# A sliding-window attention and gated MLP block: one task graph with a list scheduler in place of a hand-written order, GELU from one table function, LayerNorm by bn_stats with its small steps on GpSimd

## The chip, the cores and the metric

The kernel runs on one core of a Trainium2 chip. The core has TensorE (PE, matmuls; PEld is its weight loads), VectorE (DVE), ScalarE (ACT), GpSimd (POOL) and SyncE (SP), which here issues every transfer. Each engine works through its own queue in order and waits on semaphores for the others. The metric is device time of one execution in microseconds (us); the median of the runs shown stands for the kernel.

## What is computed

The reference, cut to what matters (S = 2048 tokens, D = 448, 16 heads of 28, F = 1792, Fh = 896; bfloat16 in and out):

```python
h  = x + A(layernorm(x))
h2 = h + B(layernorm(h))                  # the output

def A(x):                                 # 16 heads, Dh = 28, W = 8, dilation 2
    q, k, v = split(x @ wqkv)
    # query t sees keys t, t-2, ..., t-14 (those >= 0)
    logits = where(mask, einsum(q, k[window]) * Dh**-0.5, -1e9)
    return einsum(softmax(logits), v[window]) @ wo

def B(x):
    z  = gelu(x @ w_in)                   # tanh form
    z1 = z[..., :Fh]
    z2 = layernorm(z[..., Fh:])
    g  = w_sp @ z2 + b_sp[:, None]        # mixes the tokens, 2048 x 2048
    return (z1 * g) @ w_out
```

## The kernel before

Tokens lie in 16 blocks of 128 (`x_tm`, one row per token). A LayerNorm scales a block into `tring`, PE transposes it, and the result goes into `xhT` (features on the partitions). Attention runs over 18 blocks of 114 queries with 14 keys of history, so that a block's window is a band of 128 keys: logits for 16 heads into four PSUM banks (L416), exponentials on ACT (L423) into `E`, a mask by DVE (L432), the product with V and a column of ones for the denominator (L444), division (L454, L457), transpose (L472, L475), output projection and residual (L485, L488).

The order is written out by hand. First come statistics of x (L347, L348), one rsqrt chain of 16 DVE operations for eight blocks at a time (`rsqrt_chain`), scaling on DVE (L351), and the q and k projections of tokens 0 to 1023 (L383). A loop over attention blocks then interleaves logits, V, products and outputs, with two "fillers" in each round: the remaining q and k tiles and transposes. Only when all 16 blocks of h exist (its sums are collected by L488 and L491) does the second LayerNorm begin: sums to mean and variance, the rsqrt chain, 16 scalings (L351), 64 transposes (L360) with 16 copies (L369).

The MLP follows: 32 half tiles of z2 (L744), each with GELU spelled out as copy from PSUM (L708, ACT), three DVE operations (L712 to L714), a sigmoid (L718, ACT), a product with a running sum (L723, DVE) and a square with a running sum (L733, ACT). After the last of them come the third LayerNorm's chain and 16 in-place scalings of `z2p` (L787). Then 28 tiles (7 feature chunks by 4 token chunks of 512), each with z1 (L755, the same GELU with L727 at its end), 16 accumulating matmuls for g (L800), bias and product (L813, L815); behind each token chunk four output blocks (L823, L827, and the store L829). `w_sp` is held transposed as two halves of 1024 tokens: `wspT_lo` is loaded at the start (L309), `wspT_hi` where the attention's buffers were, once these are free (L668).

The class `Sched` only turns reads and writes into semaphore waits; what stands first in the program stands first in an engine's queue.

Of the kernel before, what the change touches and what calls it, by code (L numbers as in the profile page):

```python
# [1 line left out]

# [27 lines left out]
GELU_C = 0.044715  # L30
GELU_K2 = 1.5957691216057308
RSQ_MAGIC = 0x5F3759DF
# [9 lines left out]
class Res:  # L42
    __slots__ = ("name", "writes", "reads", "prewritten")

    def __init__(self, name, prewritten=False):
        self.name = name
        self.writes = {}
        self.reads = {}
        self.prewritten = prewritten


class Sched:
    EXEC_ENGS = ("pe", "act", "dve", "pool", "sp")

    def __init__(self, nc):
        self.nc = nc
# [7 lines left out]
        self.store_keys = []  # L64

    def issue(self, exe, fn, reads=(), writes=(), prod=None, inc=1):
        if prod is None:
            prod = exe
        elif prod == "dma":
            prod = "q%d" % self.ndma  # L70
            self.ndma += 1
            self.keys.append(prod)
        needed = {}
        for r in reads:
            assert r.writes or r.prewritten, "read of never-written resource " + r.name
            for e, c in r.writes.items():
                if c > needed.get(e, 0):
                    needed[e] = c
        for w in writes:
            for e, c in w.writes.items():  # L80
                if c > needed.get(e, 0):
                    needed[e] = c
            for e, c in w.reads.items():
                if c > needed.get(e, 0):
# [3 lines left out]
        for e, c in needed.items():  # L88
# [5 lines left out]
            snap = self.hist[e][c]  # L94
            for k, v in snap.items():
# [9 lines left out]
        for r in reads:  # L105
            r.reads[prod] = n
        for w in writes:
            w.writes = {prod: n}
            w.reads = {}
        self.ops[exe].append((waits, fn, prod, inc))  # L110
        return prod, n

    def wait_keys(self, exe, keys):
        self.ops[exe].append(([(k, self.cnt[k]) for k in keys], None, None, 0))

    def emit(self, exe, eng):
        sems = self.sems
        for waits, fn, prod, inc in self.ops[exe]:
            for e, c in waits:
                eng.wait_ge(sems[e], c * 16 if e.startswith("q") else c)  # L120
            if fn is None:
                continue
            ins = fn(eng)
            if prod is not None:
                ins.then_inc(sems[prod], inc)


def bass_sequential_preLN__sliding_local_dilated__mixer_gmlp__prompt_kernel(
# [11 lines left out]
    sch = Sched(nc)  # L140
    iss = sch.issue

    X = A_x[0]
    OUT = out[0]

    with contextlib.ExitStack() as top:
        def sb(name, shape, dt, es=top):
            return es.enter_context(nc.sbuf_tensor(name, shape, dt))

        x_tm = sb("x_tm", [128, NB, D], BF16)  # L150
        NTR = 8
# [4 lines left out]
        ones1 = sb("ones1", [1, 128], BF16)  # L156
        bsp = sb("bsp", [1, S_TOK], BF16)
        bb = sb("bb", [128, S_TOK], BF16)
        warm = sb("warm", [128, 512], BF16)
        mf = sb("mf", [128, 128], F32)  # L160
        ij = sb("ij", [128, 128], I32)
        pf = sb("pf", [128, 128], F32)
        st1 = sb("st1", [128, NB, 6], F32)
        mv1 = sb("mv1", [128, NB, 2], F32)
        s2a = sb("s2a", [128, NB], F32)
        s2b = sb("s2b", [128, NB], F32)
        s3a = sb("s3a", [128, 2, NB], F32)
        s3b = sb("s3b", [128, 2, NB], F32)
        junk = sb("junk", [128, 512], BF16)
        junk2 = sb("junk2", [128, 512], BF16)  # L170
        mv2 = sb("mv2", [128, NB, 2], F32)
        mv3 = sb("mv3", [128, NB, 2], F32)
        rsa = [sb("rsa%d" % i, [128, NB], F32) for i in range(4)]
        rsti = [sb("rsi%d" % i, [128, NB], I32) for i in range(4)]
        rsy = [sb("rsy%d" % i, [128, NB], F32) for i in range(4)]
        rst1 = [sb("rst%d" % i, [128, NB], F32) for i in range(4)]
        w_in = sb("w_in", [DC, NCH, F_DIM], BF16)
        wspT_lo = sb("wspT_lo", [128, NB, 1024], BF16)

# [4 lines left out]
        r_tr = [Res("tring%d" % s) for s in range(NTR)]  # L184
        r_xhT = [Res("xhT%d" % m) for m in range(NB)]
        r_xhTpad = Res("xhTpad")
# [707 lines left out]
```

## Time and profile before

| | us |
|---|---|
| median of the two runs shown | 345.44 (345.01 and 345.88) |
| span of the profiled execution, first to last instruction | 342.4 |
| median less span | 3.0 |
| mean granted TensorE clock of the profiled execution | 0.915 |

The two runs are given as whole times only; of the profiled execution the span is what is known, so the difference stands for what lies around it. The page's parts are the busy time of each engine, the span in 40 slices with the granted clock, the chain of work that ended last, and groups of instructions by source line; a table of stretches gives the same busy times between two moments, and a timeline single instructions. A name such as L744 is a line of the kernel before.

### The profile page before, as it was taken

Reading aid. Unit: us, or ns where it says so; the run is one execution under the profiler, and the core shown is the slowest. Engines: PE = TensorE matmul, PEld = TensorE weight load, DVE = VectorE, ACT = ScalarE, POOL = GpSimd, SP = SyncE. Lnnn points to the kernel's source line nnn. Section 1 sums busy time; section 2 is a strip of 40 time slices with the busy share of each in tenths; the row PEclk is TensorE's granted clock in tenths of the full one; section 3 lists DMA queues with packets and bytes.
Section 4 is the critical chain, followed back from the end, with each engine's and each line's share of the span. In section 5 each row is a group of like instructions: output and inputs, shape, how many; then the busy total and the mean of one; then the engine's idle time right before and its main releaser. Section 6 shows DMA issues by size and latency. Waiting matters only on the chain.

```text
span 342.4 us, 4998 instructions
## 1 busy us (share of the span) xinstructions
PE 287.6 (84%) x1859; PEld 144.9 (42%) x1872; DVE 242.8 (71%) x670; ACT 156.8 (46%) x320; POOL 5.1 (1%) x17
## 2 busy tenths in 40 slices
PE   3789899999998848966550099999999999999996
PEld 1434455555565617521110034444444444444442
DVE  4987446897779779899999896554555565545554
ACT  1435878777866020899999322221222022212220
POOL 5000000000000000000000000000000000000000
PEclk9879989999987556999996589999999999999999
DMA  7999900000000069930000000001000100000001
GB/s 223 258 220 179 190 16 2 2 0 2 3 2 1 2 162 187 161 76 0 0 1 1 0 2 0 0 2 50 3 3 0 38 17 0 0 26 30 1 0 54
DMA packets 40537, 16.39 MB, mean 48 GB/s; under 512 B 34177, under 2 KB 39617, under 8 KB 40514
## 3 DMA queue, kind: packets, MB, share of 16 engines
q1 hardware_dynamic: 40514, 16.08, 22.5%
q8 instruction: 14, 0.23, 0.3%
q14 instruction: 9, 0.07, 0.1%
HBM read 5.85 MB, written 1.84 MB: 22 GB/s over the span
## 4 chain that ended last, share of the span: by engine, by line
PE 66%; DVE 28%; ACT 2%; issue 2%; DMA 1%; ACTq 0%; DVEq 0%
PE psum L800 29%; PE psum L383 9%; PE psum L755 7%; PE psum L823 6%; DVE z2p L723 5%; PE psum L400 4%; PE psum L485 4%; PE psum L444 4%; DVE wk L714 3%; DVE wk L712 3%; DVE wk L713 3%; DVE xhT L369 2%; DVE tring L351 2%; PE psum L416 2%; DVE st L347 1%
## 5 line engine op out<-in xcount | busy, mean ns | idle before, releaser
L708 ACT ACTIVATE xb<-psum 128x448 bf16<-128x448 f32 (+1 forms) x60 | 33.4, 558 | 108.3 <-PE psum L755 95.5
L800 PE MATMUL psum<-wspT_lo,z2p 128*128 128x512 bf16 x217 | 52.7, 388 | 17.9 <-DVE z2p L787 17.4
L712 DVE TENSOR_TENSOR wk<-xb 128x448 bf16<-128x448 bf16 (+1 forms) x60 | 24.2, 404 | 40.1 <-ACT xb L708 40.1
L800 PE MATMUL psum<-wspT_hi,z2p 128*128 128x512 bf16 x218 | 49.7, 379 | 0.3
L423 ACT ACTIVATE E<-psum 128x456 bf16<-128x456 f32 (+1 forms) x72 | 39.6, 550 | 15.1 <-PE psum L472 8.8
L800 PEld LDWEIGHTS psum<-wspT_lo,z2p 128*128 128x128 bf16 x224 | 21.9, 98 | 46.9 <-DVE z2p L787 22.3
L718 ACT ACTIVATE tb<-wk 128x448 bf16<-128x448 bf16 (+1 forms) x60 | 35.9, 598 | 12.7 <-DVE wk L714 12.7
L744 PE MATMUL psum<-w_in,xhT 112*128 112x448 bf16 x128 | 28.7, 365 | 11.1 <-ACT xb L708 11.1
L800 PEld LDWEIGHTS psum<-wspT_hi,z2p 128*128 128x128 bf16 x224 | 21.9, 98 | 26.5
L755 PE MATMUL psum<-xhT,w_in 112*128 112x512 bf16 x112 | 28.8, 379 | 1.2 <-ACT xb L708 1.2
L714 DVE TENSOR_TENSOR wk<-wk,xb 128x448 bf16<-128x448 bf16 (+1 forms) x60 | 24.5, 408 | 2.1
L744 PEld LDWEIGHTS psum<-w_in,xhT 112*128 112x128 bf16 x128 | 11.4, 101 | 28.0 <-ACT xb L708 19.0
L444 PEld LDWEIGHTS psum<-V,E 128*114 128x114 bf16 (+1 forms) x288 | 21.4, 149 | 2.4 <-issue 0.4
L823 PE MATMUL psum<-w_out,z1p 128*128 128x448 bf16 x112 | 22.0, 353 | 0.1
L444 PE MATMUL psum<-V,E 128*114 128x29 bf16 (+1 forms) x288 | 21.7, 210 | 0.0
L485 PE MATMUL psum<-wo,OT 112*128 112x448 bf16 x64 | 18.4, 420 | 3.9 <-DVE OT L475 2.8
L432 DVE TENSOR_TENSOR E<-E,maskb 128x1824 bf16<-128x1824 bf16 (+1 forms) x18 | 19.9, 1103 | 1.8 <-ACT E L423 1.7
L813 DVE TENSOR_TENSOR ub<-psum,bb 128x512 bf16<-128x512 f32 x28 | 19.1, 683 | 2.3 <-PE psum L800 2.3
L723 DVE CUSTOM_DVE_ANT_0 z2p<-tb,xb 128x448 bf16<-128x448 bf16 x32 | 19.8, 618 | 0.9 <-ACT tb L718 0.8
L383 PE MATMUL psum<-xhT,wqp 112*128 112x512 bf16 x64 | 18.1, 440 | 2.3 <-DVE xhT L369 2.3
L827 DVE TENSOR_TENSOR tring<-psum,x_tm 128x448 bf16<-128x448 f32 x16 | 10.0, 624 | 13.5 <-PE psum L823 13.5
L713 DVE TENSOR_SCALAR wk<-wk 128x448 bf16<-128x448 bf16 (+1 forms) x60 | 17.1, 285 | 2.1
(82 smaller groups left out, 338.1 us busy)
## 6 DMA issues: line engine op xcount, KB each, us to landing
x_tm<-in_A_x_dram SPq DMA_DIRECT2D x4, 448.0 KB, 7.2
out_dram<-tring SPq DMA_DIRECT2D x16, 112.0 KB, 1.7
w_in<-in_B_w_in_dram SPq DMA_DIRECT2D x1, 1568.0 KB, 15.5
stg<-in_A_wqkv_dram SPq DMA_DIRECT2D x1, 1176.0 KB, 9.9
w_out<-in_B_w_out_dram SPq DMA_DIRECT2D x1, 784.0 KB, 4.5
wo<-in_A_wo_dram SPq DMA_DIRECT2D x1, 392.0 KB, 12.9
wspT_lo<-in_B_w_sp_dram SPq DMA_TRANSPOSE x16, 4.0
wspT_hi<-in_B_w_sp_dram SPq DMA_TRANSPOSE x16, 4.1
```

What stands on the lines that cost most here:

```text
L383: e.matmul(out_ap, wsrc[:, c, gg, :], xhT[0:DC, c, col0:col0 + 512], start=(c == 0), stop=(c == NCH - 1)),
L423: iss("act", lambda e, in_ap=in_ap, out_e=out_e: e.activation(out_e, in_ap, AF.Exp, scale=SCALE), reads=[r_bank[hh]], writes=[r_E[slot]])
L444: e.matmul(psum[0:nq, ob + h * 32: ob + h * 32 + DH + 1], E[0:nk, slot, eidx, 0:nq], V1[0:nk, vslot, h, 0:DH + 1]),
L708: iss("act", lambda e: e.activation(self.XB, self.in_ps_ap, AF.Copy), reads=[self.rbank], writes=[r_xb[s]])
L712: iss("dve", lambda e: e.tensor_tensor(self.WK, self.XB, self.XB, ALU.mult), reads=[r_xb[s]], writes=[r_wk[s]])
L714: iss("dve", lambda e: e.tensor_tensor(self.WK, self.WK, self.XB, ALU.mult), reads=[r_wk[s], r_xb[s]], writes=[r_wk[s]])
L718: iss("act", lambda e: e.activation(self.TB, self.WK, AF.Sigmoid, scale=GELU_K2), reads=[r_wk[s]], writes=[r_tb[s]])
L723: iss("dve", lambda e: e.tensor_tensor_reduce(self.out_dst_ap, self.TB, self.XB, 1.0, 0.0, ALU.mult, ALU.add, self.sum_x_ap), reads=[r_tb[ ...
L744: iss("pe", lambda e, c=c: e.matmul(out_ap, xhT[0:DC, c, PAD + 128 * m: PAD + 128 * m + 128], w_in[:, c, FH + D * k: FH + D * (k + 1)], st ...
L755: iss("pe", lambda e, c=c: e.matmul(out_ap, w_in[:, c, fc * 128:(fc + 1) * 128], xhT[0:DC, c, PAD + 512 * tc: PAD + 512 * (tc + 1)], start ...
L800: iss("pe", lambda e, sbk=sbk: e.matmul(out_ap, z2p[:, sbk, fc * 128:(fc + 1) * 128], wsrc[:, sbk, coff:coff + 512], start=(sbk == 0), sto ...
L823: iss("pe", lambda e, fc=fc: e.matmul(out_ap, z1p[:, fc, 128 * m:128 * m + 128], w_out[:, fc, :], start=(fc == 0), stop=(fc == FC7 - 1)), ...
```

## The change

Every piece of work becomes a task of a graph: alternatives of engine and duration, the buffers that it reads, writes or adds to, and a priority. `Graph.schedule` places the tasks one at a time: among the tasks whose inputs are planned it takes the engine that can start first, and on it, of those that could start within 0.05 us, the one of the lowest priority number; buffers of a pool (PSUM banks, rings) are assigned then. The queues are written in the order of the planned starts, so waits are again only semaphores, but the order comes from these durations:

```diff
+LAT = {"pe": 0.20, "act": 0.16, "dve": 0.14, "pool": 0.20, "sp": 0.0}
+TABLE_US = 1.4
...
+            eng = min(first, key=lambda e: first[e])
+            lim = first[eng] + 0.05
+            best = min((c for c in by_task.values() if c[3] == eng and c[0] <= lim), key=lambda c: (c[2].prio, c[2].idx))
...
+        def pe_us(n, cols):
+            return n * (cols / 2400.0 + 0.003)
+        def act_us(n, sbuf=False):
+            return (n + (190 if sbuf else 105)) / 1200.0
+        def dve_us(n, rate=1.0):
+            return (n / rate + 85) / 960.0
```

All three LayerNorms go block by block, by `bn_stats` and `bn_aggr` on DVE; the variance plus epsilon and its power -0.5 go to GpSimd, and for the first two LayerNorms the scaling too:

```diff
+        def layernorm(m, i, prio):
+            G.add([("dve", dve_us(D))], [lambda e: e.bn_stats(st[:, s.slot, 0:6], x_tm[:, m, :])],
...
+            rstd_of(k, prio)
...
+            G.add([("pool", 0.65)], [lambda e: e.tensor_scalar(tring[:, t.slot, :], x_tm[:, m, :], mv[:, k, 0:1],
+                                                              rstd[:, k:k + 1], ALU.subtract, ALU.mult)],
...
+            G.add([("act", act_us(512)), ("dve", dve_us(512, 2))], [evac], [b], [r_xhT[m]], prio=prio)
...
+        def rstd_of(k, prio):
+            G.add([("pool", 0.2)], [lambda e: e.tensor_scalar(va[:, k:k + 1], mv[:, k, 1:2], EPS, None, ALU.add)],
...
+            G.add([("pool", 0.3)], [lambda e: e.tensor_tensor(rstd[:, k:k + 1], va[:, k:k + 1], mhalf[:, 0:1], ALU.pow)],
-            iss("dve", lambda e: e.tensor_tensor_reduce(x_tm[:, m, :], out_ap, x_tm[:, m, :], 1.0, 0.0,
-                                                       ALU.add, ALU.add, s2a[:, m:m + 1]),
...
+            G.add([("dve", dve_us(D))], [lambda e: e.tensor_tensor(x_tm[:, m, :], bank(b, D), x_tm[:, m, :], ALU.add)],
+                  [b, r_x[m]], [r_x[m]], prio=p)
+            layernorm(m, 1, p + 0.3)
```

GELU is one ACT operation from PSUM for z2 and z1; a z2 half tile may start on PE behind the fourth-last exponential, its GELU behind the last:

```diff
-                iss("act", lambda e: e.activation(self.XB, self.in_ps_ap, AF.Copy), reads=[self.rbank], writes=[r_xb[s]])
-                iss("dve", lambda e: e.tensor_tensor(self.WK, self.XB, self.XB, ALU.mult), reads=[r_xb[s]], writes=[r_wk[s]])
...
+                    lambda e, b=b, h=h, m=m: e.activation(z2p[:, m, D * h:D * (h + 1)], bank(b, D), AF.Gelu_apprx_tanh)],
+                    [b], [r_z2[m][h]], prio=p, table="gelu", after=[last_exp])
...
+            G.add([("dve", 0.40)], [lambda e, k=k, m=m: e.tensor_scalar(z2p[:, m, :], z2p[:, m, :], mv[:, k, 0:1],
+                                                                       rstd[:, k:k + 1], ALU.subtract, ALU.mult)],
```

`E` is 128 columns wide, cleared once by GpSimd, and the product with V reads all 128. Evacuations of projections, V, transposes and attention outputs may go to ACT or DVE, as the planner finds; attention outputs overwrite `qT`. `w_sp` is held as two quarters of 512 tokens: `wsp0`, and `wsp1`, which overlays the qkv weights (`early`) and names them all as written by each load; the third and fourth quarter are loaded into the same two places when the g tiles of the first and second are done. x arrives in five loads, the qkv weights in two; the bias row is spread over the partitions by one transfer (`bb`), where PE and ACT did it.

```diff
+        def load_wsp(tc, dst, res, prio, guard=()):
+            for s in range(NB):
+                dma(lambda e, s=s: e.dma_start(dst[:, s, :], B_w_sp[512 * tc:512 * (tc + 1), s * 128:(s + 1) * 128],
+                                               transpose=True),
+                    360, reads=[], writes=[res[s]] + list(guard), prio=prio)
...
+        load_wsp(1, wsp1, r_wsp[1], 20, guard=[r_stqk, r_stv] + r_wq + r_wk)
```

How this moves the queues is shown at three places. The first is DVE in the z2 stage; before, what stands for one half tile (`xb`, `wk`, `tb`: copy, work and sigmoid tiles; `s3a`: the running sum):

```order
L712 TENSOR_TENSOR wk<-xb 128x448 [waits sem_act]
L713 TENSOR_SCALAR wk<-wk 128x448 [waits sem_dve]
L714 TENSOR_TENSOR wk<-wk,xb 128x448 [waits sem_dve]
L723 ISA z2p,s3a<-tb,xb 128x448 [waits sem_act]
L723 ISA s3a 128x1
```

Now DVE has, for two blocks (four half tiles), statistics, two aggregates and two scalings, which wait for GpSimd:

```order
L640 BN_STATS st<-z2p 128x6
L640 BN_STATS st<-z2p 128x6 [waits sem_act]
L642 BN_AGGR mv<-st 128x2 [waits sem_dve] x2
L640 BN_STATS st<-z2p 128x6 [waits sem_act] x2
L645 TENSOR_SCALAR z2p<-z2p,mv,rstd 128x896 [waits sem_pool] x2
```

The three elementwise passes and the product are gone from DVE, and the scaling of z2 moved from the end of the stage into it. On PE, behind the last half tile of z2, z1 tiles (L654) and pieces of the first g tiles (L667, four blocks of z2 at a time) alternate; the last of these rows but one is the first that waits for z2 blocks 12 to 15:

```order
L654 MATMUL psum<-xhT,w_in 128x512 [waits sem_act]
L654 MATMUL psum<-xhT,w_in 128x512 x3
L667 MATMUL psum<-wsp,z2p 128x512 [waits sem_q17,sem_q16,sem_q18,sem_q15,sem_dve]
L667 MATMUL psum<-wsp,z2p 128x512 x3
L667 MATMUL psum<-wsp,z2p 128x512 [waits sem_q21,sem_q20,sem_q22,sem_q19,sem_dve]
L667 MATMUL psum<-wsp,z2p 128x512 x7
L654 MATMUL psum<-xhT,w_in 128x512 x4
L667 MATMUL psum<-wsp,z2p 128x512 x4
L667 MATMUL psum<-wsp,z2p 128x512 [waits sem_q25,sem_q24,sem_q26,sem_q23,sem_dve]
L667 MATMUL psum<-wsp,z2p 128x512 x15
```

Before, a whole g tile followed each z1 tile. The second place is GpSimd at the start; before, its queue ended with these memsets:

```order
L322 IOTA ij 128x128
L323 MEMSET V 128x2560
L324 MEMSET xhT 112x4x14
L325 MEMSET kT 128x4x14
L326 MEMSET wqp 112x64x4
L327 MEMSET wkp 112x64x4
```

Now it goes on, after the same kinds of memsets, with E, the copies of the k weights (`early`; q2 is the load of the q and k weights), and the first LayerNorm (L512 adds epsilon, L514 is the power, L491 the scaling):

```order
L424 MEMSET V 128x512 x3
L426 MEMSET E 128x1024 x3
L475 COPY early<-early 112x16x28 [waits sem_q2]
L475 COPY early<-early 112x16x28 x3
L512 TENSOR_SCALAR va<-mv 128x1 [waits sem_dve] x2
L514 TENSOR_TENSOR rstd<-va,mhalf 128x1 [waits sem_pool] x2
L491 TENSOR_SCALAR tring<-x_tm,mv,rstd 128x448 [waits sem_pool] x2
```

The LayerNorm's small operations and scaling came onto GpSimd, behind the copies that wait for a load. The third place is SP's queue of loads; before, behind the first weights:

```order
L306 DMA w_in<-in_B_w_in_dram 112x4x1792
L307 DMA bsp<-in_B_b_sp_dram 1x2048
L309 DMA_TRANSPOSE wspT_lo<-in_B_w_sp_dram 128x1024 x16
L666 DMA w_out<-in_B_w_out_dram 128x7x448 [waits sem_pe,sem_act,sem_q2]
L668 DMA_TRANSPOSE wspT_hi<-in_B_w_sp_dram 128x1024 x16
```

Now, with the first three of the second quarter's sixteen loads (`early`):

```order
L456 DMA w_out<-in_B_w_out_dram 128x7x448
L460 DMA_TRANSPOSE wsp<-in_B_w_sp_dram 128x512 x16
L460 DMA_TRANSPOSE early<-in_B_w_sp_dram 128x512 [waits sem_pe]
L460 DMA_TRANSPOSE early<-in_B_w_sp_dram 128x512 [waits sem_q27]
L460 DMA_TRANSPOSE early<-in_B_w_sp_dram 128x512 [waits sem_q28]
```

The w_out load moved ahead of the w_sp loads, and each load of the second quarter waits for the one before it, where the second half's loads were issued in a row.

More of the change, by code (lines that the diff above doesn't have):

```diff
@@ L1 @@
 import contextlib
+import heapq
 import concourse.bass as bass
@@ L855, in bass_sequential_preLN__sliding_local_dilated__mixer_gmlp__prompt_kernel, with phys @@
+        def phys(rs):
+            return [r.pool.res[r.slot] if isinstance(r, Buf) else r for r in rs]
+        store_ids = {t.idx for t in stores}
+        store_keys = []
+        for t in order:
+            key = sch.issue(t.eng, t.fns, phys(t.reads), phys(t.writes), phys(t.adds))
+            if t.idx in store_ids:
+                store_keys.append(key)
+        nc.sched_order = order
         for name in sch.keys:
```

1135 lines of the change are left out of this document (486 added, 649 removed).

## The prediction

> **What bounds the kernel now.** I read the page first (busy shares, the 40 slices), then the chain of waits, which says where the order changes hands, then the table of stretches cut at those places, then single rows.
>
> ```profile
> span 342.4 us, 4998 instructions
> PE 287.6 (84%) x1859; PEld 144.9 (42%) x1872; DVE 242.8 (71%) x670; ACT 156.8 (46%) x320; POOL 5.1 (1%) x17
> PE 66%; DVE 28%; ACT 2%; issue 2%; DMA 1%; ACTq 0%; DVEq 0%
> ```
>
> No engine is full over the span, and POOL (GpSimd) is empty. The chain is two thirds PE and a quarter DVE (VectorE), so the bound changes with the stage. The table of stretches (columns: stretch, length, then busy us and instructions of PE, weight loads, DVE, ACT, POOL, then granted clock, DMA share, GB/s) shows where:
>
> ```profile
> 18.50:38.00 19.50, 18.86 (x105) 8.73 (x106) 13.85 (x50) 10.48 (x18) 0.00 (x0) 0.91 1.03 193
> 38.00:111.90 73.90, 69.19 (x807) 42.98 (x806) 55.23 (x122) 55.44 (x105) 0.00 (x0) 0.92 0.09 15
> 111.90:138.00 26.10, 19.15 (x127) 12.99 (x127) 21.36 (x76) 2.93 (x5) 0.00 (x0) 0.57 0.61 123
> 138.00:190.00 52.00, 28.35 (x131) 10.88 (x128) 48.74 (x160) 51.02 (x127) 0.00 (x0) 0.93 0.24 35
> 190.00:195.10 5.10, 0.00 (x0) 0.00 (x0) 3.69 (x22) 1.55 (x4) 0.00 (x0) 0.50 0.00 0
> 195.10:342.40 147.30, 142.59 (x651) 64.67 (x664) 86.76 (x200) 30.28 (x54) 0.00 (x0) 0.99 0.04 13
> ```
>
> Up to 111.9 (projections and attention) PE is busy 94%. From 111.9 to 195.1 it is not the bound: first the last attention blocks and the second LayerNorm run serially at a granted clock of 0.57, then GELU of z2 fills DVE and ACT (ScalarE) for 52 us around 28 us of PE work, then the third LayerNorm leaves PE with nothing. From 195.1 PE is full at a clock of 0.99. So 83 of 342 us are not bound by matmuls, and these the change attacks.
>
> **The change, part by part.** The sum goes against the profiled execution's own span, 342.4; the median of the runs shown, 345.44, is 3.0 us above it, and I add that 3.0 at the end. I cut at three events: first projection matmul (18.5), last mask of E (rows below: 110.89 + 1.06 = 112.0), z2 normalized (195.1).
>
> *1. Start to the first projection.*
>
> ```profile
> 0.41 0.10 POOL L879 MEMSET const-uint8-127<- 128x1 uint8 x1
> 1.08 0.29 POOL L313 TENSOR_SCALAR_AFFINE_SELECT ident<-ident 128x128 bf16<-128x128 bf16 x1
> 2.97 2.23 POOL L323 MEMSET V<- 128x2560 bf16 x1
> 4.16 0.63 DVE L347 BATCH_NORM_STATS2 st<-x_tm 128x6 f32<-128x448 bf16 x1 [4.16 <-DMA x_tm<-in_A_x_dram]
> x_tm<-in_A_x_dram SPq DMA_DIRECT2D x4, 448.0 KB, 7.2
> stg<-in_A_wqkv_dram SPq DMA_DIRECT2D x1, 1176.0 KB, 9.9
> 11.79 0.58 ACT L334 ACTIVATE wqp<-stg 112x448 bf16<-112x448 bf16 x1 [4.81 <-DMA stg<-in_A_wqkv_dram]
> 18.50 5.30 PE L383 MATMUL psum<-xhT,wqp 112*128 112x512 bf16 x16 [1.72 <-DVE xhT L369]
> ```
>
> POOL's new queue is: constants, four V and three E memsets, four copies of the k weights (behind the weights' DMA), and only then the first LayerNorm. The V row gives 0.87 ns an element, so the memsets are 7.5 to 10 us of work (E counted as 1024 words or as 2048 elements). The first weights were there at 11.79 as the end of 2.07 MB (two x loads and stg); now they are the end of 1.03 MB (a quarter of that x and two thirds of stg), some 7 to 10 us. A POOL pass over 448 elements has no row: 448 at the memset's rate is 0.4 us, the 0.29 us of the 128-column select scaled by 3.5 is 1.0; I take 0.8. The four copies are then 1.6 to 4 us, four LayerNorms with two small operations each (0.10 to 0.29 apiece) 2.4 to 6.4, transposing and evacuating about 1. That spans 13 to 22 us; the middle is 18. DVE's rsqrt chain, which stood there, falls out. I take no change; ends -4 and +4.
>
> *2. Attention up to the last mask.* PE gets the 64 transposes of the second LayerNorm, which stood behind 123 us, and shorter weight loads, since E is now read 128 columns wide.
>
> ```profile
> 103.96 0.22 PEld L416 LDWEIGHTS psum<-qT,kT 32*128 32x128 bf16 x16 [0.37 <-ACT V L403]
> 103.97 0.38 PE L416 MATMUL psum<-qT,kT 32*128 32x114 bf16 x16
> 104.47 0.92 PEld L444 LDWEIGHTS psum<-V,E 128*114 128x114 bf16 x16
> 104.52 0.97 PE L444 MATMUL psum<-V,E 128*114 128x29 bf16 x16
> 41.95 0.45 PE psum L360 x8
> ```
>
> Eight transposes took 0.45 in the chain, so 64 take 3.6, with handovers some 5 us. Sixteen loads of 128 columns took 0.22 us where sixteen of 114 took 0.92, and the pairs took 0.38 and 0.97: up to 0.59 x 18 blocks = 10.6 us off PE, none if something else paces. I take half, 5: the two cancel. (The Trainium skill, "TensorE: Matmul & The Clock Gate", Weight-path perf modes, says that loads go by a faster path when there are exactly 128 weights and the type isn't FP32; the rows agree, and by that rule alone the sum would get the whole 10.6.) DVE loses the scaling of both LayerNorms and the sums (L491, L488 with its read of the accumulator), and gets statistics of the same length; ACT and DVE share the evacuations. The stretch rows give both some 55 of 74 us, so there is room. Qk projections of tokens 512 to 1023 move behind the first logits, which start earlier by as much. Last mask at 112; ends -8 (PE paces alone, 10.6 gained) and +12 (work of three engines that don't mesh, 10% of the 94 us from 18 to 112, with a few us of contention).
>
> *3. From the last mask to z2 normalized, now 83.1 us.* The serial LayerNorm chain, the sums and the 15 us of transposing go into the attention. GELU becomes one ACT operation per half tile in place of copy, three DVE operations, sigmoid, product and square.
>
> ```profile
> 110.89 1.06 DVE L432 TENSOR_TENSOR E<-E,maskb 124x1760 bf16<-124x1760 bf16 x1
> 186.91 0.62 DVE L723 CUSTOM_DVE_ANT_0 z2p<-tb,xb 128x448 bf16<-128x448 bf16 x1
> 188.49 0.62 DVE L723 CUSTOM_DVE_ANT_0 z2p<-tb,xb 128x448 bf16<-128x448 bf16 x1
> L347 DVE BATCH_NORM_STATS2 st<-x_tm 128x6 f32<-128x448 bf16 x16 | 10.0, 626 | 4.8 <-DMA x_tm<-in_A_x_dram 4.2
> L348 DVE BATCH_NORM_AGGREGATE mv<-st 128x2 f32<-128x6 f32 x16 | 2.9, 182 | 0.6
> L787 DVE TENSOR_SCALAR z2p<-z2p,mv,rst 128x896 bf16<-128x896 bf16 x16 | 6.9, 506 | 0.0
> L827 DVE TENSOR_TENSOR tring<-psum,x_tm 128x448 bf16<-128x448 f32 x16 | 10.0, 624 | 13.5 <-PE psum L823 13.5
> L369 DVE COPY xhT<-psum 112x512 bf16<-112x512 bf16 x32 | 11.3, 412 | 5.8 <-PE psum L360 5.8
> L454 DVE RECIPROCAL rcp<-psum 114x16 f32<-114x16 f32 (+1 forms) x18 | 4.6, 256 | 9.0 <-PE psum L444 8.9
> L708 ACT ACTIVATE xb<-psum 128x448 bf16<-128x448 f32 (+1 forms) x60 | 33.4, 558 | 108.3 <-PE psum L755 95.5
> L744 PE MATMUL psum<-w_in,xhT 112*128 112x448 bf16 x128 | 28.7, 365 | 11.1 <-ACT xb L708 11.1
> ```
>
> Today a half tile costs 1.58 us (188.49 - 186.91) of DVE. Behind the last mask DVE's new queue holds 36 statistics, 20 aggregates, 16 scalings, four residual adds and the last attention blocks' two reciprocals, two products and five copies. By durations: 36 x 0.626 + 20 x 0.182 + 16 x 0.506 + 4 x 0.624 = 36.8, and the last nine at 2 x 0.256, 2 x 0.624 and 5 x 0.41 make 3.8; 40.6. By starts, which overlap by 0.08 or so (the product at 188.49 is followed 0.54 later), about 36. I take 39, nearer the durations, since many of these wait for DVE's own result. ACT has 32 GELUs of about 0.6 (L708's 0.558 with a gap; the table's function itself has no row) and one table load as before, 21; PE 24. So DVE stays the bound of this stage, for 39 instead of 83 us. The rstd comes from POOL: for two blocks two adds and two powers, while DVE has two statistics (1.25 us) to do. At 0.10 to 0.29 apiece that is 0.4 to 1.2, hidden; with waits on top the end is +4, and -3 for the starts.
>
> *4. From z2 normalized to the end, now 147.3.*
>
> ```profile
> L755 PE MATMUL psum<-xhT,w_in 112*128 112x512 bf16 x104 | 26.7, 378 | 0.0
> 206.70 0.86 PE psum L755 x4
> 211.89 3.46 PE psum L800 x16
> 232.62 5.30 PE psum L823 x28
> L309 SPq DMA_TRANSPOSE wspT_lo<-in_B_w_sp_dram x16: 1298/1301/5924, 10.9 to 40.2; - x16
> DMA to landing us min/median/max: 3.6/4.0/12.0
> ```
>
> The first row is from the groups of 196 to 336 us: 104 of 112 z1 matmuls, so two tiles of z1 ran earlier. PE has 26 x 0.86 + 28 x 3.46 + 4 x 5.30 = 140.4, and it bounds. DVE's and ACT's removed GELU work costs and saves nothing here, as PE covers it (they are busy 87 and 30 of 147 us); without that cover it would save up to 1.58 us a tile again. The bias row, now spread by a DMA instead of four matmuls and copies, is an early load with over 100 us to land: nothing. PE's new order puts three z1 tiles and 20 g matmuls ahead of the wait for the last z2 blocks, so one more tile and 20 x 0.216 = 4.3: 5.2 us done in the gap of stage 3. The tail saves about 0.6, since only the seventh product of each output block waits for the last z1. The w_sp quarters are loaded again while others are used: 16 transposes of 1.30 to issue and 4.0 to land are 25 us, under a chunk of 7 x 4.32 + 5.3 = 35.5 us; the last four stores stand behind them, not ahead. But the second quarter overlays the qkv weights, and its 16 loads each wait for the one before (guard in the code): from the last V projection, about 107, they need 16 x 3.6 to 4.0, with a wake-up 60 to 66 us, done at 167 to 173. PE asks for the last at 151 + 20 + 4 + 5 + 3.5 = 183. Hidden with 10 us to spare; ends 0 and +5. So 147.3 - 5.2 - 0.6 = 141.5.
>
> **Sum**: 112 + 39 + 141.5 = 292.5, and 3.0 outside the span: 295.5, say 295.
>
> **The rivals.**
> - *The order does not mesh*: it is laid out for durations that are too short for ACT (act_us counts 0.47 us for an exponential; the row below has 0.55). Then engines wait for each other at every block, +10 us: 305. For it: with the second LayerNorm moved in, all three have more of this stage to fill. Against: the stretch rows show 94%, 75% and 75% busy side by side already.
> ```profile
> L423 ACT ACTIVATE E<-psum 128x456 bf16<-128x456 f32 (+1 forms) x72 | 39.6, 550 | 15.1 <-PE psum L472 8.8
> ```
> - *POOL and DVE hold each other up.* Twenty-eight scalings of 0.4 to 1.0 us that DVE sits out are 11 to 28 us, less the 18 it has free in attention: 0 to +10; near the upper end, 303. No row of before shows both at work. (The Trainium skill, "GPSIMD Engine Reference", Key points, speaks against the change: the engine shares its SBUF interfaces with VectorE and is about half as fast at elementwise work; no run here shows either yet, and by it this rival would be the likeliest.)
> - *The power is slow*: at 0.8 us for each small POOL operation, four need 3.2 against 1.25 us covered: 2 x 8 pairs = 16, and 4 at the start: 315.
> - *The serial loads are late*: above 4.7 us apiece ((183 - 107) / 16) PE waits. At 6 it is +20: 315.
> - *PE paces alone in attention*, with the full gain of the weight loads: 287, or less with an early start.
> - *Slower than before*: POOL paces everything. It has 32 LayerNorms before z2 is complete. To end above 352 the last must be 57 us later, at 112 + 57: (169 - 10) / 32 = 5.0 us per LayerNorm, where I count 1.4. Only a power of some 4 us decides that, against rows of 0.1 to 0.3.
>
> **How the numbers follow.** A measurement of this kernel tells about 2% (7 us) from no change. The forecast (295) 47%; the order 15%; POOL against DVE 13%; PE alone 12%; slow power 6%; late loads 4%; slower 3%. Range 281 to 312: below it lies a start 4 us early together with the whole of PE's gain, above it most of the slow power, the late loads and the slower case, about 2 in 10 with the tails of the rest. Faster by 2% holds in all cases but the last and an extreme power: 0.95; within 0.02; slower 0.03.
>
> **What the profile after would show.** Right: DVE over 85% busy from the last mask to the last z2 scaling, that stretch 36 to 43 us; PE full at a clock of 0.99 behind it; no rstd wait over 0.5 us on DVE; E's weight loads at or below 0.10 us. Wrong: PE waiting for the second w_sp quarter; POOL rows for the scaling far from 0.8, or DVE rows that grow beside them (mask above 1.1 us); the last mask later than 124; a granted clock below 0.9 in attention.

## The result and the profile after

The changed kernel took 304.20 us (median of 2 runs, 302.17 and 306.23), the kernel before 345.44 beside it: a ratio of 0.8875 with a 95% interval of 0.8517 to 0.9234. A repetition later (`e0_after_again`, 4 runs against 7) gave 303.98 and 0.8893, 0.8830 to 0.8956; its four spans are 300.2, 301.4, 303.1 and 307.4 us, the longest at a granted clock of 0.915 where the others had 0.953 or 0.954. The profiled execution is the one at 302.17 us, with a span of 300.5.

The page of the changed kernel: the busy shares, the granted clock over 40 slices, the chain by engine and by line.

```profile
span 300.5 us, 4652 instructions
PE 268.0 (89%) x1868; PEld 133.9 (45%) x1868; DVE 153.1 (51%) x321; ACT 102.2 (34%) x193; POOL 111.9 (37%) x155
PEclk9879998799999965899999999999999999999999
PE 55%; POOL 29%; DVE 9%; DMA 2%; issue 2%; ACT 0%; DVEq 0%; SPq 0%; POOLq 0%
PE psum L667 31%; POOL tring L491 18%; POOL rstd L514 8%; PE psum L654 7%; PE psum L685 7%; POOL va L512 3%; PE psum L596 3%; DVE st L640 2%; PE psum L496 2%; DMA early<-in_A_wqkv_dram 2%; PE psum L524 2%; DVE z2p L645 2%; DVE st L486 1%; PE psum L547 1%; DVE x_tm L599 1%
```

DVE's share fell from 71 to 51%, as its GELU passes went. But the chain now runs through GpSimd for 29% of the span, although that engine is busy only 37% of it: over the whole span it is not full, but it is waited for. The stretches between the first projection, the last mask of E and the end of the last z2 scaling (columns: stretch, length, busy us and instructions of PE, weight loads, DVE, ACT, POOL, then granted clock, DMA share, GB/s):

```profile
0.00:21.70 21.70, 13.88 (x57) 6.26 (x58) 14.93 (x37) 5.54 (x9) 20.93 (x43) 0.84 0.96 242
21.70:120.75 99.05, 82.16 (x943) 45.97 (x943) 63.76 (x128) 59.69 (x120) 68.28 (x69) 0.90 0.18 38
120.75:161.80 41.05, 36.55 (x233) 19.30 (x231) 33.96 (x86) 22.01 (x39) 22.66 (x44) 0.99 0.19 43
161.80:300.50 138.70, 135.40 (x640) 62.39 (x640) 40.50 (x73) 14.93 (x25) 0.00 (x0) 1.00 0.19 44
```

The prediction calls 195.1 the moment at which z2 is normalized in the kernel before. It is the moment at which the chain of the third LayerNorm is done and the first of its 16 scalings starts; the last one starts at 201.4 and ends at 201.9. The line of the scalings before (shortest, median and longest in ns, first and last start in us):

```profile
L787 DVE TENSOR_SCALAR z2p<-z2p,mv,rst x16: 503/506/513, 195.1 to 201.4; 128x896 bf16<-128x896 bf16 x16
```

Compared by the same event, the stage to normalized z2 was 89.9 us before, not 83.1, and the rest 140.5, not 147.3.

Before, PE was busy 94% of projections and attention; now 83%, and part of that at half clock. The groups and waits that say why, from the page and from PE's own waits (us in total, times, longest):

```profile
L491 POOL TENSOR_SCALAR tring<-x_tm,mv,rstd 128x448 bf16<-128x448 bf16 x32 | 63.5, 1988 | 3.8 <-PE psum L496 2.8
L514 POOL TENSOR_TENSOR rstd<-va,mhalf 128x1 f32<-128x1 f32 x48 | 28.8, 610 | 1.4
L512 POOL TENSOR_SCALAR va<-mv 128x1 f32<-128x1 f32 x48 | 11.1, 244 | 43.4 <-DVE mv L488 31.1
PE psum L496 <- POOL tring L491: 25.3, 18, 4.0
```

A LayerNorm on GpSimd costs 1.87 (the median, below) + 0.57 + 0.23 us or so, 2.7, where the prediction counted 1.4. PE stands still 18 times until a scaled block comes to be transposed (L496). The second half of attention shows how that becomes a chain; pieces of the chain of waits in order of time, start and length:

```profile
101.50 0.64 DVE x_tm L599
102.16 0.63 DVE st L486
103.41 0.58 POOL rstd L514
104.08 1.88 POOL tring L491
106.43 0.77 PE psum L596 x4
107.23 0.64 DVE x_tm L599
107.89 0.63 DVE st L486
109.13 0.58 POOL rstd L514
109.80 2.52 POOL tring L491
112.37 0.67 PE psum L496 x4
```

PE's queue is in order, and the planner, counting on 0.65 us, put the transposes of one block (L496) ahead of the output projection of the next (L596). So each block's residual, statistics, power and scaling follow one another, some 5.7 us a round (107.23 - 101.50), and PE waits before the transposes (1.17 us until 106.0, 1.58 until 112.4).

### The profile page after: what moved, and what is told of

It reads as the page before. It is cut to its first block, busy times and chain, and to the rows that moved or that the text cites. A ratio compares the mean times of both kernels' runs of the same rounds, so it can differ in the third digit from the quotient of the medians.

```text
span 300.5 us, 4652 instructions
## 1 busy us (share of the span) xinstructions
PE 268.0 (89%) x1868; PEld 133.9 (45%) x1868; DVE 153.1 (51%) x321; ACT 102.2 (34%) x193; POOL 111.9 (37%) x155
## 4 chain that ended last, share of the span: by engine, by line
PE 55%; POOL 29%; DVE 9%; DMA 2%; issue 2%; ACT 0%; DVEq 0%; SPq 0%; POOLq 0%
PE psum L667 31%; POOL tring L491 18%; POOL rstd L514 8%; PE psum L654 7%; PE psum L685 7%; POOL va L512 3%; PE psum L596 3%; DVE st L640 2%; PE psum L496 2%; DMA early<-in_A_wqkv_dram 2%; PE psum L524 2%; DVE z2p L645 2%; DVE st L486 1%; PE psum L547 1%; DVE x_tm L599 1%
## 5 line engine op out<-in xcount | busy, mean ns | idle before, releaser
L491 POOL TENSOR_SCALAR tring<-x_tm,mv,rstd 128x448 bf16<-128x448 bf16 x32 | 63.5, 1988 | 3.8 <-PE psum L496 2.8
L659 ACT ACTIVATE z1p<-psum 128x512 bf16<-128x512 f32 x28 | 16.7, 597 | 114.8 <-PE psum L654 114.8
L667 PE MATMUL psum<-wsp,z2p 128*128 128x512 bf16 x224 | 51.2, 379 | 0.5 <-DVE z2p L645 0.5
L667 PE MATMUL psum<-early,z2p 128*128 128x512 bf16 x224 | 50.8, 379 | 0.0
L496 PE MATMUL psum<-ident,tring 128*112 128x128 bf16 x128 | 15.2, 250 | 25.3 <-POOL tring L491 25.3
L667 PEld LDWEIGHTS psum<-wsp,z2p 128*128 128x128 bf16 x224 | 21.8, 98 | 27.2 <-DVE z2p L645 0.9
L667 PEld LDWEIGHTS psum<-early,z2p 128*128 128x128 bf16 x224 | 21.9, 98 | 26.4
L524 PE MATMUL psum<-xhT,early 112*128 112x512 bf16 x128 | 31.1, 379 | 0.0
L514 POOL TENSOR_TENSOR rstd<-va,mhalf 128x1 f32<-128x1 f32 x48 | 28.8, 610 | 1.4
L654 PE MATMUL psum<-xhT,w_in 112*128 112x512 bf16 x112 | 28.8, 378 | 0.0
L512 POOL TENSOR_SCALAR va<-mv 128x1 f32<-128x1 f32 x48 | 11.1, 244 | 43.4 <-DVE mv L488 31.1
L496 PEld LDWEIGHTS psum<-ident,tring 128*112 128x112 bf16 x128 | 11.4, 149 | 33.8 <-POOL tring L491 32.0
L509 DVE COPY xhT<-psum 112x512 bf16<-112x512 bf16 x19 | 7.9, 420 | 28.3 <-PE psum L496 28.3
L486 DVE BATCH_NORM_STATS2 st<-x_tm 128x6 f32<-128x448 bf16 x32 | 18.9, 611 | 1.3 <-DMA x_tm<-in_A_x_dram 1.0
L535 PE MATMUL psum<-early,xhT 112*128 112x448 bf16 (+1 forms) x72 | 19.2, 404 | 0.0
L640 DVE BATCH_NORM_STATS2 st<-z2p 128x6 f32<-128x448 bf16 x32 | 17.9, 600 | 0.0
```

Source lines behind the costliest of these rows:

```text
L486: G.add([("dve", dve_us(D))], [lambda e: e.bn_stats(st[:, s.slot, 0:6], x_tm[:, m, :])], [r_x[m]], [s], [s], prio=prio)
L491: G.add([("pool", 0.65)], [lambda e: e.tensor_scalar(tring[:, t.slot, :], x_tm[:, m, :], mv[:, k, 0:1], rstd[:, k:k + 1], ALU.subtract, AL ...
L496: lambda e, c=c: e.transpose(psb[0:DC, b.slot * 1024 + c * 128: b.slot * 1024 + c * 128 + 128], tring[:, t.slot, c * DC:(c + 1) * DC], ide ...
L512: G.add([("pool", 0.2)], [lambda e: e.tensor_scalar(va[:, k:k + 1], mv[:, k, 1:2], EPS, None, ALU.add)], [r_mv[k]], [r_va[k]], prio=prio)
L514: G.add([("pool", 0.3)], [lambda e: e.tensor_tensor(rstd[:, k:k + 1], va[:, k:k + 1], mhalf[:, 0:1], ALU.pow)], [r_va[k], r_half], [r_rs[k ...
L524: lambda e, c=c: e.matmul(bank(b, 512), wsrc[:, c, gg, :], xhT[0:DC, c, col0:col0 + 512], start=(c == 0), stop=(c == NCH - 1)) for c in ra ...
```

## The experiments

Two theories: **A**, GpSimd's scaling is slow and its duration costs; **B**, the order, planned on wrong durations, makes the engines wait. Each ratio is against runs of the kernel before on the same chip; the medians of different rows of the table come from up to four such sessions, in which the kernel before itself lay between 340.77 and 345.44, so medians that differ by a few us are not told apart. Stages by the same four events, in us of span (first q or k projection, last mask of E done, end of the last z2 scaling, end); the prediction's row is its own sum, whose last two stages were taken against 83.1 and 147.3:

| kernel | to first projection | attention | to z2 normalized | to the end | span | median of runs |
|---|---|---|---|---|---|---|
| before | 18.5 | 93.5 | 89.9 | 140.5 | 342.4 | 345.44 |
| predicted | 18.5 | 93.5 | 39 | 141.5 | 292.5 | 295 |
| changed | 21.7 | 99.1 | 41.1 | 138.7 | 300.5 | 304.20 |
| e5, old order with the new GELU | 18.5 | 90.2 | 59.5 | 140.5 | 308.7 | 312.51 |
| e11, scaling planned at 1.87 | 22.9 | 84.4 | 36.4 | 137.8 | 281.4 | 282.83 |
| e6, same order, scaling run on DVE | 20.9 | 80.8 | 36.3 | 138.7 | 276.6 | 277.81 |
| e1, scaling planned and run on DVE | 17.7 | 81.7 | 34.6 | 136.2 | 270.2 | 272.11 |

**The change once more.**

> The changed kernel again, as the base that the others of this call are set against. Its profiled span was 300.5 us. Every theory: 298 to 304 us of span. It also tells how far two executions differ, since the two times shown lie 4 us apart.

It repeated: ratio 0.8893, 0.8830 to 0.8956. Three of the four spans lie within the 298 to 304 expected, the fourth is 307.4.

**GELU alone** (`e5_gelu_only`): the kernel before with its hand-written order, GELU from the table and statistics for z2 by `bn_stats`.

```diff
-                iss("act", lambda e: e.activation(self.XB, self.in_ps_ap, AF.Copy), reads=[self.rbank], writes=[r_xb[s]])
+                iss("act", lambda e: e.activation(self.out_dst_ap, self.in_ps_ap, AF.Gelu_apprx_tanh), reads=[self.rbank],
+                    writes=[self.rdst])
...
-                iss("dve", lambda e: e.tensor_tensor(self.WK, self.XB, self.XB, ALU.mult), reads=[r_xb[s]], writes=[r_wk[s]])
...
+                iss("dve", lambda e: e.bn_stats(self.sum_x_ap, self.out_dst_ap), reads=[self.rdst], writes=[self.rsx])
```

> The kernel before with its hand-written order, and of the change only GELU from the table and statistics of z2 by bn_stats (the third LayerNorm's chain stays at the end of the stage). If the removed DVE work carries the z2 stage: 52 us of the stage become 26 to 30 (PE 24, ACT 20), span 316 to 322, which leaves 16 to 22 us of the whole gain to the new order. If the stage is then held by the hand-overs between PE and ACT or by the chain at its end: 35 us or more, span 327 or more.

312.51 us, ratio 0.9172 (0.9102 to 0.9243); the span of the profiled execution fell by 33.7 to 308.7, below both forecasts. By the table 30.4 of this are in the z2 stage and nothing behind it; the 3.3 in attention, where the instructions are the same, go with a clock of 0.96 in place of 0.92 and are no work of GELU's. The scalings of z2 in this run, whose end the table takes:

```profile
161.34 6.86 DVE L772 TENSOR_SCALAR z2p<-z2p,mv,rst 128x896 bf16<-128x896 bf16 x16
```

Of the change's 41.9 us of span, 30 to 34 are to be had by this part alone (28.3 of 36.8 by the medians of one session); all the rest, the task graph with LayerNorm on GpSimd, added some 8.

**Scaling on DVE** (`e1_scale_dve`) and **the measured durations in the plan** (`e2_durations`):

```diff
-            G.add([("pool", 0.65)], [lambda e: e.tensor_scalar(tring[:, t.slot, :], x_tm[:, m, :], mv[:, k, 0:1],
+            G.add([("dve", 0.40)], [lambda e: e.tensor_scalar(tring[:, t.slot, :], x_tm[:, m, :], mv[:, k, 0:1],
```

> The scaling of the first two LayerNorms on DVE (planned at 0.40 us) instead of GpSimd; rstd stays on GpSimd; the planner orders again. Theory A (GpSimd's scaling, 1.87 us each, is what made the start and the attention 8.7 us longer than summed): first projection at 16 to 18 us instead of 21.7, last mask at 111 to 115 instead of 120.8, span 290 to 295. Rival B (three engines don't mesh because the plan's durations are wrong, whoever scales): span within 3 us of the changed kernel, 297 to 303.

```diff
-            G.add([("pool", 0.65)], [lambda e: e.tensor_scalar(tring[:, t.slot, :], x_tm[:, m, :], mv[:, k, 0:1],
+            G.add([("pool", 1.87)], [lambda e: e.tensor_scalar(tring[:, t.slot, :], x_tm[:, m, :], mv[:, k, 0:1],
...
-            G.add([("pool", 0.3)], [lambda e: e.tensor_tensor(rstd[:, k:k + 1], va[:, k:k + 1], mhalf[:, 0:1], ALU.pow)],
+            G.add([("pool", 0.55)], [lambda e: e.tensor_tensor(rstd[:, k:k + 1], va[:, k:k + 1], mhalf[:, 0:1], ALU.pow)],
...
-            return (n + (190 if sbuf else 105)) / 1200.0
+            return (n + (190 if sbuf else 260)) / 1200.0
```

> The same engines as the changed kernel, but the planner gets the durations that the trace shows (GpSimd scaling 1.87, power 0.55, ACT 0.13 us more, aggregate 0.18, z2 scaling 0.50, product with V 0.6). Only the order changes. Theory A: GpSimd still has 32 x 2.6 us to do, so at most 4 us are won, span 297 to 302. Rival B: the wrong durations cost the 8 us, span 293 or less.

With the scaling on DVE: 272.11 us, ratio 0.7991 (0.7941 to 0.8041), a span of 270.2, which is below what either theory expected. With it on GpSimd but these durations in the plan true (the warm-up matmuls at 8.0 in place of 6.0 us are among them): 284.69, ratio 0.8348 (0.8302 to 0.8393), a span of 283.8, as rival B expected and beyond the 4 us that theory A allowed. Each run thus speaks for its own theory, with an effect larger than thought, and neither excludes the other, since in the first the planner ordered anew too: the next runs take them apart. Against `e5`, the task graph with the scaling on DVE is worth 38.5 us of span (308.7 to 270.2), not 8.

**The old plan run on DVE** (`e6_plan_pool_run_dve`):

```diff
+            swap.append(sc)
...
         order = G.schedule()
+        for t in swap:
+            t.eng = "dve"
```

> The changed kernel's plan, in which the LayerNorm scaling stands on GpSimd at 0.65 us, is kept; only when the queues are written out is each of the 32 scalings put into VectorE's queue, at its planned start. Theory 1 (the scaling's 1.9 us on GpSimd is what costs, the order is sound): with the scaling at some 0.35 us the same order gives the time of the version planned for VectorE, 270 to 277 us. Theory 2 (the order, laid out with durations that are wrong, costs by itself, and planning anew is what helped in the other runs): the queues now hold 32 operations on VectorE that the plan did not count there, and the time stays above 284.

277.81 us, ratio 0.8112 (0.8059 to 0.8164), 0.8 us above theory 1's range and far below theory 2's: with a fast scaling the same order is nearly sound, and re-planning for DVE brings the last 6.4 us of span. The attention stretch of this run beside the changed kernel's, and the scaling's own rows, of the changed kernel and of this run:

```profile
20.88:101.70 80.82, 75.82 (x965) 43.91 (x963) 70.53 (x155) 59.74 (x122) 13.35 (x33) 1.00 0.29 45
```

```profile
L491 POOL TENSOR_SCALAR tring<-x_tm,mv,rstd x32: 1853/1872/2822, 11.6 to 134.7; 128x448 bf16<-128x448 bf16 x32
```

```profile
L493 DVE TENSOR_SCALAR tring<-x_tm,mv,rstd x32: 305/388/397, 13.6 to 111.8; 128x448 bf16<-128x448 bf16 x32
```

The stretch shrank by 18.2 us (99.05 to 80.82): PE's idle time by 11.9 (16.89 to 5.00) and its busy time by 6.3 (82.16 to 75.82) for nearly as many recorded matmuls (943 and 965), at a clock of 1.00 in place of 0.90. The clock of the changed kernel, cut finer:

```profile
98.00:102.00 4.00, 3.66 (x52) 2.31 (x52) 2.24 (x4) 1.49 (x3) 0.29 (x1) 1.00 0.00 0
106.00:110.00 4.00, 3.84 (x60) 2.49 (x61) 2.60 (x6) 2.92 (x6) 0.99 (x3) 0.77 0.00 0
110.00:114.00 4.00, 2.42 (x28) 1.65 (x27) 2.03 (x5) 1.87 (x4) 2.31 (x1) 0.50 0.14 33
118.00:121.00 3.00, 3.00 (x13) 1.51 (x12) 2.94 (x5) 1.11 (x3) 1.85 (x1) 0.50 0.05 12
```

So a third of the loss is not waiting but slower matmuls: the clock fell to 0.50 soon after a wait of PE for GpSimd (1.17 us, up to 106.0) and stayed there to 121, while in `e6`, with most of the waiting gone, it was 1.00 over the whole stretch. Which gaps bring it down is not shown: from 66 to 82 us PE was busy 11.82 of 16 us at a clock of 1.00. (The Trainium skill, "TensorE: Matmul & The Clock Gate", Part 1, says that the clock is halved when PE has been idle over a window and is released by activity, with nothing between; the rows of 0.50 and 1.00 agree, and a 0.77 is a stretch with both. That PE idled over such a window no row shows: from 98 us to the fall its longest wait is the 1.17 us.)

**The scaling's duration alone in the plan** (`e11_plan_scale_only`): of `e2`'s edits only the scaling's line.

> The changed kernel with its scaling on GpSimd, and of all durations in the plan this one alone set to what was measured, 1.87 in place of 0.65 us. Theory 1 (of the eight durations changed together in the run at 284.7 us, the scaling's is the one that counted): 283 to 289 us. Theory 2 (ScalarE's and the small GpSimd operations' durations, too short in the plan, were the greater part): 294 to 302 us.

282.83 us, ratio 0.8222 (0.8159 to 0.8285): 0.2 below theory 1's range and far from theory 2's, and no slower than `e2` with all eight durations true. One number in the plan, with the same slow instruction on the same engine, is worth 19.1 us of span (300.5 to 281.4). What the planner does with it, on GpSimd and PE, by the lines of the run:

```profile
L491 POOL TENSOR_SCALAR tring<-x_tm,mv,rstd 128x448 bf16<-128x448 bf16 x32 | 61.6, 1928 | 2.5 <-PE psum L496 1.3
PE psum L496 <- POOL tring L491: 6.2, 4, 2.9
```

GpSimd's scalings are busy 61.6 us where they were 63.5, but PE waits for them 6.2 instead of 25.3 us: a plan that knows when the scaled block comes puts its transposes where other matmuls fill the time. This and `e6` overlap: the one hides the slow operation, the other removes it, and their gains don't add up.

**Other durations, with the scaling on DVE** (`e3_dve_durations`): `e1` with the remaining edits of `e2`.

> Scaling on VectorE as in the run at 272.1 us, and the planner gets the measured durations for the rest (power 0.55 us, ScalarE's operations 0.13 us longer, aggregate 0.18, z2 scaling 0.50, the product with V 0.6). Theory 1 (only GpSimd's scaling was priced far enough off to matter): 271 to 274 us. Theory 2 (the order gains from each true duration): 265 to 269 us.

273.25 us, ratio 0.7975 (0.7922 to 0.8028): theory 1. ScalarE's rate, too short by 0.13 us an operation, did no harm.

**A free choice of engine** (`e14_either`):

```diff
-            G.add([("pool", 0.65)], [lambda e: e.tensor_scalar(tring[:, t.slot, :], x_tm[:, m, :], mv[:, k, 0:1],
+            G.add([("pool", 1.87), ("dve", 0.40)], [lambda e: e.tensor_scalar(tring[:, t.slot, :], x_tm[:, m, :], mv[:, k, 0:1],
```

> The planner may put each scaling on GpSimd at 1.87 us or on VectorE at 0.40 us, whichever ends earlier; it leaves 3 of 32 on GpSimd. Theory 1 (every scaling on GpSimd costs where VectorE and the matmuls wait for it): no better than all on VectorE, 271 to 276 us. Theory 2 (a few on GpSimd relieve VectorE, which is over 90% busy in the first third): 266 to 270 us.

273.40 us, ratio 0.7963 (0.7886 to 0.8041): theory 1, no gain over DVE alone.

**Narrow weight loads of E** (`e8_dve_narrow_E`): `e1`, with this edit (the product's output rows, `psum[0:nq, ...]` in place of `psum[:, ...]`, go with it and are left out here):

```diff
-                                                E[0:nk, ev.slot, hh * 4 + g, :], V1[0:nk, v.slot, 4 * g + hh, 0:DH + 1])
+                                                E[0:nk, ev.slot, hh * 4 + g, 0:nq], V1[0:nk, v.slot, 4 * g + hh, 0:DH + 1])
```

> Scaling on VectorE as in the run at 272.1 us; the product with V reads E in 114 columns as the kernel before did, so each of the 288 weight loads takes the slower path (149 instead of 98 ns in the groups; 0.97 instead of some 0.4 us for sixteen). Theory 1 (PE paces the attention there, so the weight loads are on the path): 18 blocks by up to 0.59 us, 277 to 282 us. Theory 2 (something else paces the attention and the wide loads were worth nothing): 271 to 274 us.

275.55 us, ratio 0.8052 (0.8001 to 0.8103), between the two theories and not told apart from `e1` by the intervals. The attention stretches of `e1` and, below it, of this run show what the medians leave open:

```profile
17.68:99.40 81.72, 78.72 (x976) 45.34 (x975) 73.17 (x162) 65.03 (x132) 19.12 (x44) 1.00 0.28 56
```

```profile
18.50:103.40 84.90, 84.23 (x976) 53.48 (x975) 73.76 (x162) 65.20 (x132) 19.14 (x44) 1.00 0.28 51
```

The narrow loads add 5.5 us of PE work and 3.2 us to the stretch; the rest went into the 3.0 us that PE had sat idle there. That is one profile each.

**GpSimd's memsets and DVE's cast.** In the changed kernel DVE's cast of the integer mask took 3.36 us, against 0.23 before (where it ran at 32 us, with no memset beside it), and ended with GpSimd's memsets of E; the timelines of DVE and GpSimd (start, length):

```profile
4.59 3.36 DVE L430 CAST z2p<-z2p 128x128 f32<-128x128 int32 x1
```

```profile
5.14 2.74 POOL L426 MEMSET E<- 128x1024 f32 x3
```

First attempt (`e10_dve_memset_late`): `e1`, with the memsets of E named behind the cast (`masks[1]`):

```diff
+            G.add([("pool", 0.9)], [lambda e, s=s: e.memset(E[:, s].bitcast(F32), 0.0)], writes=[P_E.res[s]], prio=-40, after=[masks[1]])
```

> Scaling on VectorE as in the run at 272.1 us; the three memsets of E on GpSimd wait until VectorE's cast of the integer mask is done. Theory 1 (VectorE's cast took 3.4 to 3.6 us because GpSimd's memsets ran beside it, and it holds up the first LayerNorms): the cast takes below 0.5 us, the first projection comes 1 to 3 us earlier than 17.7 us, and the time is 269 to 271 us. Theory 2 (the cast is slow by itself): it still takes over 3 us, and the time is 271 to 275 us.

272.96 us and a cast of 3.59: nothing learned, for `after` orders tasks in the plan only and emits no semaphore; the memsets ran beside the cast as ever. Second attempt (`e12_dve_memset_waits`), with a wait:

```diff
+            G.add([("pool", 0.9)], [lambda e, s=s: e.memset(E[:, s].bitcast(F32), 0.0)], reads=[r_mask], writes=[P_E.res[s]], prio=-40)
```

> Scaling on VectorE as in the run at 272.1 us; the three memsets of E on GpSimd now read the finished mask, so that a semaphore holds them back (the earlier attempt ordered them in the plan only, and they ran beside the cast as before). Theory 1 (VectorE's cast took 3.6 us because GpSimd's memsets ran beside it): only the last V memset is left beside it, and the cast ends within 0.5 us of that memset's end at 5.2 us, under 1.3 us in all. Theory 2 (the cast of 128x128 integers is slow here by itself): over 3 us again. For the time both expect 269 to 274 us, since the memsets then stand behind the cast in GpSimd's queue.

270.39 us, ratio 0.7855 (0.7776 to 0.7934). That is 0.6% below `e1`, from another session, in which the kernel before took 344.84 us against 340.77, and the two profiled spans are 270.0 and 270.2: no gain in time is shown, though the first projection came at 16.7 in place of 17.7 us. The timelines of GpSimd and of DVE in this run (start, length):

```profile
3.74 1.45 POOL L424 MEMSET V<- 128x512 bf16 x3
6.60 2.73 POOL L435 MEMSET E<- 128x1024 f32 x3
```

```profile
4.68 0.59 DVE L427 CAST z2p<-z2p 128x128 f32<-128x128 int32 x1
6.28 3.17 DVE L491 TENSOR_SCALAR tring<-x_tm,mv,rstd 128x448 bf16<-128x448 bf16 x2
```

Theory 1: away from the memsets of E the cast is short. The hold-up moved on to the two scalings that now fall beside those memsets: 3.17 us for a pair whose single one has a median of 0.39, and they end at 9.45 with the memsets at 9.33.

## Why the prediction was right, and where it was off

The time, 304, lies in the range of 281 to 312, and faster was right. That the sum came so near is in part luck: the work in attention was priced too high by 13 us and GpSimd's scaling too low by more than that, and a base that was read wrongly made up for a part of the rest. Step by step:

1. *Start.* Forecast no change, measured +3.2 us. The step that was mis-sized is the price of GpSimd's scaling: "448 at the memset's rate is 0.4 us, the 0.29 us of the 128-column select scaled by 3.5 is 1.0; I take 0.8". It measured 1.87, outside both ends; a copy of 448 columns on GpSimd took 0.59 (median). So neither a memset nor a select nor a copy is near to this operation, which also reads two operands of one element per partition. The start is GpSimd's queue, here with PE's rows beside it:

```profile
8.00 2.20 POOL L475 COPY early<-early 112x448 bf16<-112x448 bf16 x4
11.62 3.74 POOL L491 TENSOR_SCALAR tring<-x_tm,mv,rstd 128x448 bf16<-128x448 bf16 x2
16.77 3.74 POOL L491 TENSOR_SCALAR tring<-x_tm,mv,rstd 128x448 bf16<-128x448 bf16 x2
15.88 3.19 PE L535 MATMUL psum<-early,xhT 112*128 112x448 bf16 x8
20.83 0.92 PE L535 MATMUL psum<-early,xhT 112*128 112x448 bf16 x4
21.69 3.63 PE L524 MATMUL psum<-xhT,early 112*128 112x512 bf16 x16
```

The memsets end at 7.9 us, the copies take 2.2 (forecast 1.6 to 4), four LayerNorms 10.3 (10.2 to 20.5; forecast 2.4 to 6.4), and transposing and evacuating 1.2. Four times the missing 1.07 us is 4.3 by itself. But the time is not all lost: 12 V matmuls (L535, 4.1 us) are done ahead of the first q and k projection, where the kernel before has none. They also tell why `e6`, which takes only the scaling's time away, starts just 0.8 earlier: DVE has scaled the fourth block there at 17.1, but PE's planned order still has the 12 V matmuls ahead, and the first projection comes at 20.9. With a new plan (`e1`, eight V matmuls ahead) it came 4.0 earlier.

2. *Attention.* Forecast 93.5, measured 99.1. The same mis-sized term: `e6` puts 18.2 us on the scaling alone (the power, 0.57 for up to 0.29, stayed on GpSimd in it), and with it gone the stage takes 80.8, below the lower end of -8. So the work was priced too high by 13, some 4 of it the V matmuls that had moved ahead of the cut, and the scaling too low by 18: two errors that hid each other. I left GpSimd out of this stage's sum altogether, counting room on DVE and ACT only. Of the weight loads I credited "half, 5"; `e8` shows 5.5 us of PE work and 3.2 of time where PE nearly bounds, and none can show where it waits for GpSimd.
3. *z2.* Forecast 39, measured 41.1. GELU from the table cost 0.543 us (I took 0.6). That DVE alone binds was not right: it is busy 83%, under the 85% I named, and PE 89%, with 36.6 us of work where I counted 24, since the last attention blocks, three z1 tiles and 20 g matmuls stand there too. Of the 4.5 us that PE sat idle, 4.1 were waits for GpSimd's scaling; in `e6` the stage takes 36.3, and in `e1` 34.6 with PE at 99% (34.31 us) and DVE at 94%. DVE's two waits for rstd, 2.8 us together, were longer than the 0.5 I allowed each.
4. *To the end.* Forecast 141.5, measured 138.7, PE busy 98% at a clock of 1.00. The base of 147.3 was read wrongly: it holds the 16 scalings (195.1 to 201.9), which my sum for z2 has as well, so they were counted twice. From the end of the scalings the base is 140.5. The order came as forecast, three z1 tiles and 20 g matmuls ahead of the last scaling; but two z1 tiles and 15 g matmuls stood ahead of it before, so that 1.9 us are new (0.86 and 5 x 0.216). With the 0.6 of the tail, which no row shows by itself, that gives 138.0. The serial loads of the second quarter were issued from 110.4 on in 41.65 us, 2.6 apiece and not 3.6 to 4.0, done near 154 and first used at 191.4: hidden by 37 us, not 10.

Of the rivals, *the order does not mesh* named the right mechanism by the wrong duration: not ScalarE's (`e3`: no difference) but that of GpSimd's scaling (`e11`: 19 us); that its 305 is near the measured 304 is chance. *POOL and DVE hold each other up* is small in attention: the mask kept 1.10 us, and the scaling's mean is 0.12 us above its median (1.87, the longest 2.82), some 4 us over 32. *The power is slow* needed 0.8 us for each small operation; they took 0.57 and 0.23. *POOL paces everything* needed 5.0 us per LayerNorm and got 2.7; it did pace PE up to 50 us, as the stretch of the changed kernel from 40 to 50 shows, with GpSimd busy 9.73 of 10 us and PE 7.36.

```profile
40.00:50.00 10.00, 7.36 (x90) 4.21 (x88) 7.41 (x17) 6.33 (x13) 9.73 (x10) 1.00 0.18 41
```

The kernel before and the changed kernel are both beaten by `e1` and its variants, at 270 to 276 us. Left open: which gaps bring the matmul clock down, and whether a LayerNorm wholly on DVE, the power too, would gain; neither was tried.

## What to carry to other kernels

An engine that a plan loads newly needs its prices measured with the very operation, operands included; a price from another kind of operation on it can be off by more than twice. In a plan that orders in-order queues, a duration that is too short costs more than the operation itself: the waiting instruction holds up everything behind it, and here the matmul clock fell as well (0.90 over the attention, 1.00 in `e6`, with most of the waits gone). A stage's base and its forecast have to end at the same event, or work that moves is counted twice. Check such a plan by correcting one duration at a time, since the one that counts may be a single number.

## What the hardware showed that I had not expected

GpSimd's scaling of 128x448 with two operands of one element per partition took 1.87 us, DVE's 0.39: a factor of 4.8. (The Trainium skill, "GPSIMD Engine Reference", Key points, has about 2 for elementwise work; here the measurement decides.) A power of one element per partition took 0.57 us. The same section of the Trainium skill says that GpSimd contends with DVE where DVE runs in a two-port mode or has two inputs in SBUF, which fits the cast and the scalings that ended with the memsets; that these ran in such a mode no run here shows. Beside memsets that ran back to back DVE's cast took 3.36 us for 0.23. And GELU from the table cost what a plain copy of that size costs, 543 ns beside 548 in the changed kernel:

```profile
L637 ACT ACTIVATE z2p<-psum 128x448 bf16<-128x448 f32 x32 | 17.3, 543 | 10.9 <-PE psum L632 10.9
L508 ACT ACTIVATE V<-psum 128x448 bf16<-128x448 f32 x9 | 4.9, 548 | 6.4 <-PE psum L535 6.0 <-PE psum L569 0.3
```
